# Four of 32 weight tiles converted in the first feed-forward block instead of in the last two attention pairs

## The chip, the cores and the metric

The kernel runs on one core of a Trainium2 chip. The metric is the device time of one execution in microseconds, as the median of several runs. TensorE (PE in the profile) multiplies matrices, VectorE (DVE), ScalarE (ACT) and GpSimd (POOL) do elementwise work, and SyncE (SP) issues nearly all DMA transfers. Each engine works off its own list of instructions in order.

## What is computed

Attention with a bucket mask over 4 batches, 8 heads, 768 positions and a head size of 64, followed by a feed-forward part with a rational function in place of an activation:

```python
mask = q_bucket[:, :, :, None] == k_bucket[:, :, None, :]
scores = np.where(mask, scale * np.matmul(q, k.transpose(0, 1, 3, 2)), -1000000000.0)
attn = np.exp(scores - np.max(scores, axis=-1, keepdims=True))
attn = attn / (np.sum(attn, axis=-1, keepdims=True) + 1e-09)
x = np.matmul(attn, v)            # put together to 3072 tokens x 512

h = x @ w_in                      # 512 x 2048
P = a[0] + a[1] * h + a[2] * h * h + a[3] * h * h * h
Q = 1.0 + np.abs(b[0]) * np.abs(h) + np.abs(b[1]) * h * h
out = (P / (Q + 1e-6)) @ w_out    # 2048 x 512
```

The two weight matrices arrive as 64-bit floating-point numbers. q, k, v and the rest are 32-bit.

## The kernel before

**Attention.** The 32 heads of all batches are worked off as 16 pairs. For each pair TensorE computes the row maxima (tile psm), which VectorE reduces (m); the maxima are transposed (pst) and moved as one more row into the operand q, so that they are subtracted within the product. Then come the scores (pss), their exponentials on ScalarE (E), partial sums of the exponentials on GpSimd (acc; in the last pair partly on VectorE), the sums (psu) and the product with the values (psv). The order of all of this is written out: a table `plan` gives each piece a position, 12 positions to a pair, and the pieces are emitted in the order of these positions. Since every instruction is pinned in program order, that order is the order of each engine's list and of SP's list of transfers.

**Weights.** The two matrices are cut into 32 tiles of 128 x 512. Tile n with an even number is a piece of w_in: (n/2) divided by 4 gives the column block and the row block. Tile n with an odd number is the row block (n-1)/2 of w_out. Every tile has to be turned from 64-bit into 32-bit numbers and then split into a high part, in the reduced format that TensorE multiplies at full speed, and a low part, the rest. `weights(i)` (line 432) does it in steps: a load of 512 KB into wr; a ScalarE copy of the upper words to ws; a ScalarE copy of the lower words together with a VectorE instruction that keeps the sign; a VectorE instruction that shifts and joins; a VectorE addition (in the profile a custom instruction on 128 x 1024 half words); a ScalarE copy that gives the high part; a VectorE subtraction that gives the low part. The parts of w_in stay on the chip, in wi_hi and wi_lo. Those of w_out are stored to the tensor wo_d in HBM (a seventh or eighth step) and fetched later. Lines 522 to 527 spread these steps over the plan, two tiles to a pair of heads; tiles 28 and 29 stand in pair 14, 30 and 31 in pair 15, partly in the pair behind. Tile 31 has four closer positions for its last steps (`weights_last`, line 47).

**Tokens.** `Tokens.load` (line 637) fetches the attention's outputs for one block of 512 tokens in three chunks c, multiplies them by the reciprocals of the sums (y = x * r on VectorE) and splits the result into high and low parts (xh on ScalarE, xl on VectorE). y lies in the places lo0 and lo1 in turn. A block's tokens are made in the block before; in step f = 3, 7, 11 a chunk is loaded, two steps later y is computed and one step after that xh and xl.

**Feed-forward part.** Six blocks of 512 tokens, 16 column tiles f each: 96 steps. `Ffn.step(i)` (line 748) emits, for step i, the first product of tile i (psh, 12 matmuls), the polynomials of tile i (`terms`: three ScalarE and three VectorE instructions), the quotient of tile i-1 (`quotient`: two and three), the split of tile i-2 (`parts`: gh on ScalarE, gl on GpSimd) and the second product of tile i-4 (`gemm2`, pso, 12 matmuls: for each of four row blocks gh with the high part of the weights, gh with the low part, gl with the high part). psh has four places, and gh and gl have three each.

Steps 0 to 2 of the first block are emitted within the plan, at the end of attention. `Ffn.rest` (line 761) emits what is left. It sets up 16 places wo0 to wo15 for the tiles of w_out, in memory that attention has used, issues the loads of wo0 to wo5, and then in each step i from 3 on one load more (wo6 in step 3, wo15 in step 12). In steps 3, 6 and 7 it also advances the last store of sums and the last reciprocals.

Of the kernel before, what the change touches and what calls it, by code (L numbers as in the profile page):

```python
# [18 lines left out]
P = 128  # L19
# [80 lines left out]
    (queue or nc.sync).dma_start(out.bitcast(F32), in_.bitcast(F32))  # L100


@with_exitstack
def bucket_attention_then_rational_ffn(ctx, tc, qT, kT, v, proj, w_in, w_out, coef, consts, out):
    nc = Ordered(tc)
    nc.scalar.preload_act_table_set("natural_log_exp_and_others")

    cpool = ctx.enter_context(tc.tile_pool(name="cpool", bufs=1))
    dpool = ctx.enter_context(tc.tile_pool(name="dpool", bufs=1, space=DRAM))
    wpool = ctx.enter_context(tc.tile_pool(name="wpool", bufs=1))  # L110


    raw = ctx.enter_context(tc.tile_pool(name="raw", bufs=2))
    ps_b = ctx.enter_context(tc.tile_pool(name="ps_b", bufs=1, space=PSUM))
    QF, KF = {}, {}
# [24 lines left out]
    r_d = [dpool.tile([2 * NHP, S], F32, name=f"r_d{i}") for i in range(B)]  # L140

    wo_d = [dpool.tile([P, 2, DM], F32R, name=f"wo_d{i}") for i in range(NFC)]

    wi_hi = wpool.tile([P, NCC, DFF], F32R, name="wi_hi")
    wi_lo = wpool.tile([P, NCC, DFF], F32R, name="wi_lo")

    tokens = Tokens(tc, nc, raw, x_d, r_d)
    gemm = Gemm1(nc, ps_b, tokens, wi_hi, wi_lo)
    tail = ctx.enter_context(tc.tile_pool(name="tail", bufs=1))

    def coefficients():
        nc.sync.dma_start(ab, coef)
        yield
        nc.scalar.activation(absb1, b1, AF.Abs)
        yield

    early = ExitStack()
    right = ctx.enter_context(ExitStack())
    ffn = Ffn(tc, nc, tokens, gemm, wo_d, (a0, a1, a2, a3, b0, absb1, qbias), tail, out)
# [13 lines left out]
def attention(ctx, tc, nc, raw, ps_b, tail, tokens, early, operands_to_terms, ffn, load, QF, KF, v, w_in, w_out, wo_d, ident, cst, ones, prj,  # L173
# [256 lines left out]
        yield  # L430

    def weights(i):

        if i % 2 == 0:
            f, cc = divmod(i // 2, 4)
            sl = slice(f * 512, f * 512 + 512)
            src, hi, lo = w_in[cc * P : cc * P + P, sl], wi_hi[:, cc, sl], wi_lo[:, cc, sl]
        else:  # L440
            src, hi, lo = w_out[i // 2 * P : i // 2 * P + P, :], None, None
        r = sm.tile([P, 2 * 512], F32, tag="wr", name=f"wr{i}", bufs=2)
        t = sm.tile([P, 512], F32, tag="ws", name=f"ws{i}", bufs=2)
        if src.dtype == F32:
            nc.sync.dma_start(t, src)
            yield
        else:
            nc.sync.dma_start(r.bitcast(I32), src.bitcast(I32))
            yield
            hw, lw = r[:, 1:1024:2], r[:, 0:1024:2]  # L450
            nc.scalar.activation(t, hw, AF.Copy, scale=2.0 ** -112)
            yield
            nc.scalar.activation(lw.bitcast(I32), lw.bitcast(U32), AF.Copy, scale=2.0 ** -29)
            nc.vector.tensor_scalar(out=hw.bitcast(I32), in0=hw.bitcast(I32), scalar1=-(1 << 31), scalar2=None,
                                    op0=ALU.bitwise_and)
            yield
            nc.vector.scalar_tensor_tensor(out=t.bitcast(I32), in0=t.bitcast(I32), scalar=3, in1=hw.bitcast(I32),
                                           op0=ALU.logical_shift_left, op1=ALU.bitwise_or)
            yield
            nc.vector.tensor_tensor(out=t.bitcast(I32), in0=t.bitcast(I32), in1=lw.bitcast(I32), op=ALU.add)  # L460
            yield
        if hi is None:
            hi, lo = r[:, 0:512].bitcast(F32R), r[:, 512:1024].bitcast(F32R)
        nc.scalar.copy(hi, t)
        yield
        nc.vector.tensor_tensor(out=lo, in0=t, in1=hi.bitcast(F32), op=ALU.subtract)
        yield
        if i % 2 == 1:
            move(nc, wo_d[i // 2], r.rearrange("p (t c) -> p t c", t=2))
            yield  # L470

# [11 lines left out]
    for p in range(NPAIR):  # L483
# [133 lines left out]
class Tokens:  # L617
# [19 lines left out]
    def load(self, t, c):  # L637
        nc = self.nc
        hi, lo = self.place(t, c, "h"), self.place(t, c, "l")
        w = hi.shape[1]  # L640
        x, r = lo.bitcast(F32), hi.bitcast(F32)
        o = 0
        while o < w:
            cc, k = divmod(c * S + o, NTK)
            bb, a = divmod(t * NTK + k, S)
            n = min(S - a, NTK - k, w - o)
            nc.sync.dma_start(x[:, o : o + n], self.x_d[bb * NHP + cc][:, a : a + n])
            for j in range(2):
# [12 lines left out]

class Ffn:
# [1 line left out]

    LAG = 4

    def __init__(self, tc, nc, tokens, gemm, wo_d, coef, rows, out):
        self.tc, self.nc, self.tokens, self.gemm, self.wo_d, self.coef, self.out = tc, nc, tokens, gemm, wo_d, coef, out
        self.rows = rows
        self.state, self.sums = {}, {}  # L670
        self.done = 0
# [89 lines left out]
    def rest(self, ctx, last):  # L761
# [70 lines left out]
```

## Time and profile before

| | us |
|---|---|
| runs of the kernel | 930.82, 931.18, 933.48; median 931.18 |
| the profiled execution | 931.52 |
| its span, first to last instruction | 929.7 |
| TensorE busy | 920.8 |
| VectorE busy | 840.8 |
| ScalarE busy | 647.7 |
| GpSimd busy | 436.5 |

The granted TensorE clock is 1.00. Attention fills the span up to about 401 us and the feed-forward part the rest. "Busy" for TensorE includes overlaps of matmuls that follow each other, so its share doesn't say that TensorE works at its peak. The profile gives line 93, that of the helper which pins the order, for nearly all instructions; groups are told apart by their tiles (psh is the first product, pso the second, and so on). Views by time give the start, the duration, the engine and the group, and in brackets how long the engine had been idle and what ended it.

### The profile page before, as it was taken

How to read it: one execution, taken by the hardware profiler on the slowest of the kernel's cores; microseconds unless marked ns; L12 is line 12 of the kernel's file. 1: busy time of each engine (PE TensorE's matmuls, PEld its weight loads, DVE VectorE, ACT ScalarE, POOL GpSimd, SP SyncE). 2: the span in 40 equal slices, each digit the busy share in tenths (PEclk: the TensorE clock that was granted, in tenths of full speed). 3: DMA queues.
4: the chain of work that ended last, by engine and by line, in shares of the span. 5: the costliest groups of instructions: out<-in, count | busy, mean ns of one | idle time of the engine just before them, and what ended most of it. 6: DMA issues, size and time to landing. Idle time of an engine off the chain costs nothing.

```text
span 929.7 us, 13698 instructions
## 1 busy us (share of the span) xinstructions
PE 920.8 (99%) x4678; PEld 699.3 (75%) x4678; DVE 840.8 (90%) x1029; ACT 647.7 (70%) x1229; POOL 436.5 (47%) x362
## 2 busy tenths in 40 slices
PE   8999999999999999999999999999999999999997
PEld 4666766666767676668888888888888888888886
DVE  6799889788988897887998999999999989998996
ACT  7567767676767676886777667776676677677664
POOL 5587878777878877622222232222223222222222
PEclk9999999999999999999999999999999999999999
DMA  6867877887877777545402100400040003001001
GB/s 197 213 182 225 229 221 230 214 232 220 232 218 220 220 193 228 166 158 189 165 1 86 51 1 1 136 1 0 1 137 1 1 38 98 1 1 46 1 1 46
DMA packets 51242, 111.57 MB, mean 120 GB/s; under 512 B 9346, under 2 KB 20214, under 8 KB 51172
## 3 DMA queue, kind: packets, MB, share of 16 engines
q1 hardware_dynamic: 50740, 110.47, 40.2%
q8 instruction: 37, 0.61, 0.3%
q14 instruction: 33, 0.27, 0.1%
q10 hardware_dynamic: 432, 0.23, 0.1%
HBM read 56.82 MB, written 21.17 MB: 84 GB/s over the span
## 4 chain that ended last, share of the span: by engine, by line
PE 92%; DVE 3%; DMA 3%; SPq 1%; issue 1%; ACT 1%; DVEq 0%; ACTq 0%
PE psh L93 28%; PE pso L93 28%; PE pss L93 13%; PE psv L93 12%; PE psm L93 7%; PE psu L93 2%; DVE m L93 2%; PE psb L93 1%; SPq L93 1%; DMA wr<-w_in 1%; DMA q<-q 1%; DVE ws L93 1%; DVE wr L93 0%; DMA qkf<-kT 0%; DMA xh<-r_d 0%
## 5 line engine op out<-in xcount | busy, mean ns | idle before, releaser
L93 POOL TENSOR_TENSOR gl<-c,gh 128x512 fp32r<-128x512 f32 x96 | 134.6, 1402 | 388.3 <-ACT gh L93 378.9
L93 ACT ACTIVATE E<-pss 128x384 f32<-128x384 f32 x384 | 167.7, 493 | 104.3 <-PE pss L93 93.8
L93 PE MATMUL pso<-wo,gh 128*128 128x512 f32 x768 | 235.5, 389 | 0.0
L93 DVE TENSOR_REDUCE m<-psm 128x1 f32<-128x768 f32 x192 | 179.4, 948 | 30.7 <-PE psm L93 27.6
L93 POOL TENSOR_TENSOR acc<-E,E 128x384 f32<-128x384 f32 x124 | 154.1, 1261 | 84.5 <-ACT E L93 84.4
L93 PE MATMUL pss<-q,k 128*128 128x384 f32 (+2 forms) x768 | 171.2, 346 | 0.4 <-ACT E L93 0.3
L93 PEld LDWEIGHTS pso<-wo,gh 128*128 128x128 f32 x768 | 144.1, 188 | 29.9
L93 PEld LDWEIGHTS pss<-q,k 128*128 128x128 f32 (+2 forms) x768 | 134.5, 189 | 29.2 <-issue 17.0
L93 PE MATMUL psh<-xh,wi_hi 128*128 128x512 f32 x384 | 149.6, 390 | 0.0
L93 PE MATMUL psh<-xl,wi_hi 128*128 128x512 f32 x384 | 149.4, 389 | 0.0
L93 PE MATMUL psh<-xh,wi_lo 128*128 128x512 f32 x384 | 149.4, 389 | 0.0
L93 PE MATMUL pso<-wo,gl 128*128 128x512 f32 x384 | 148.4, 389 | 0.0
L93 ACT ACTIVATE h<-psh 128x512 f32<-128x512 f32 x96 | 57.4, 598 | 127.5 <-PE psh L93 127.4
L93 POOL TENSOR_TENSOR acc<-acc,E 128x384 f32<-128x384 f32 x123 | 137.5, 1137 | 8.2 <-ACT E L93 8.0
L93 DVE SCALAR_TENSOR_TENSOR c<-c,ab,r 128x512 f32<-128x512 f32 x96 | 135.6, 1413 | 0.0
L93 PE MATMUL psv<-E,v 128*64 128x385 f32 x768 | 133.0, 492 | 0.0
L93 PE MATMUL psm<-k,q 76*128 76x384 f32 (+1 forms) x384 | 102.1, 349 | 1.9 <-DVE m L93 1.0
L93 PEld LDWEIGHTS psv<-E,v 128*64 128x64 f32 x768 | 52.4, 136 | 66.3 <-issue 63.2
L93 DVE SCALAR_TENSOR_TENSOR w<-h,absb,w 128x512 f32<-128x512 f32 x96 | 74.0, 771 | 16.1 <-ACT w L93 15.9
L93 PEld LDWEIGHTS psh<-xh,wi_hi 128*128 128x128 f32 x384 | 72.0, 187 | 16.2 <-issue 1.2
L93 PEld LDWEIGHTS psh<-xl,wi_hi 128*128 128x128 f32 x384 | 72.1, 188 | 15.0
L93 PEld LDWEIGHTS pso<-wo,gl 128*128 128x128 f32 x384 | 72.1, 188 | 15.0
(79 smaller groups left out, 1219.4 us busy)
## 6 DMA issues: line engine op xcount, KB each, us to landing
q<-q SPq DMA_DIRECT2D x45, 192.0 KB
k<-k SPq DMA_DIRECT2D x45, 192.0 KB
wr<-w_in SPq DMA_DIRECT2D x16, 512.0 KB
wr<-w_out SPq DMA_DIRECT2D x16, 512.0 KB
wo_d<-wr SPq DMA_DIRECT2D x16, 512.0 KB
wo<-wo_d SPq DMA_DIRECT2D x16, 512.0 KB
qkf<-qT SPq DMA_DIRECT2D x16, 384.0 KB
qkf<-kT SPq DMA_DIRECT2D x16, 384.0 KB
```

The source lines that it names most:

```text
L93: return self.tc.keep_in_program_order(issue(*args, **kwargs))
```

## The change

Tiles 28 to 31 (the last two row blocks of w_in in its last column block, and the last two row blocks of w_out) are no longer in attention's plan. The body of `weights` becomes a function `convert`, used in both places. In `Ffn.rest` a table gives the steps in which the pieces of the four tiles are emitted, behind the step's own work: for tile 28 the load ahead of step 3 (behind the loads of wo0 to wo5), the first copy in step 3, and so on to the subtraction in step 7; tile 30 in steps 4 to 10, tile 29 in 7 to 13, tile 31 in 8 to 15. The tables hold one number for each of the seven pieces: load, copy, lower words and sign, join, addition, high part, low part.

The 64-bit words lie in places of w_out tiles that come later: 28 and 29 in wo15, 30 and 31 in wo13. The 32-bit numbers lie in lo1 (28 and 31), wo14 (30) and wo12 (29); lo1 is free since y now lies in lo0 always. The low part is computed on GpSimd instead of VectorE. Tiles 29 and 31 are written straight into wo14 and wo15 and aren't stored to wo_d, which has 14 tiles now. wo6 to wo11 are loaded in steps 3 to 8 as before, wo12 and wo13 in step 14 (before: steps 9 and 10).

```diff
-    weights_last=[0.5, 0.8, 1.0, 1.2],
...
+def convert(nc, src, hi, lo, buffers, kept=None, last=None):
+    r, t = buffers()
...
+    nc.scalar.copy(hi, t)
+    yield
+    (last or nc.vector).tensor_tensor(out=lo, in0=t, in1=hi.bitcast(F32), op=ALU.subtract)
+    yield
+    if kept is not None:
+        move(nc, kept, r.rearrange("p (t c) -> p t c", t=2))
+        yield
...
-    for i in range(2 * NFC):
+    for i in range(2 * NFC - 4):
         o = 12 * (i // 2)
         w = list(FIRST["weights"][i]) if i < 2 else list(MID["weights"][i % 2])
-        if i == 2 * NFC - 1:
-            w = w[:-4] + [w[-5] + x for x in MID["weights_last"]]
         spread(0, [o + x for x in w], weights(i))
...
-        y = self.raw.tile([P, w], F32, tag=f"lo{c % 2}", name=f"y{t}_{c}", bufs=1)
+        y = self.raw.tile([P, w], F32, tag="lo0", name=f"y{t}_{c}", bufs=1)
...
-        self.wo = [wp.tile([P, 2, DM], F32R, name=f"wo{i}") for i in range(NFC)]
-        AHEAD = 6
+        self.wo = {}
+
+        def second(f):
+            self.wo[f] = wp.tile([P, 2, DM], F32R, tag=f"wo{f}", name=f"wo{f}")
+            return self.wo[f]
+
+        def late(n, r, t):
+            def buffers():
+                return (wp.tile([P, 2 * 512], F32, tag=f"wo{r}", name=f"wr{n}"),
+                        tokens.raw.tile([P, 512], F32, tag="lo1", name=f"ws{n}", bufs=1) if t is None else
+                        wp.tile([P, 512], F32, tag=f"wo{t}", name=f"ws{n}"))
+
+            if n % 2 == 0:
+                yield from convert(nc, *parts_of_w_in(n // 2, self.w_in, self.gemm.hi, self.gemm.lo), buffers, last=nc.gpsimd)
+            else:
+                yield from convert(nc, self.w_out[n // 2 * P : n // 2 * P + P, :], lambda: second(n // 2), None, buffers, last=nc.gpsimd)
+
+        AHEAD, LATE = 6, {}
+        for n, r, t, steps in ((28, 15, None, (2, 3, 4, 4, 5, 6, 7)), (30, 13, 14, (4, 6, 7, 7, 8, 9, 10)),
+                               (29, 15, 12, (7, 9, 10, 10, 11, 12, 13)), (31, 13, None, (8, 11, 12, 12, 13, 14, 15))):
+            g = late(n, r, t)
+            for i in steps:
+                LATE.setdefault(i, []).append(g)
         for f in range(AHEAD):
-            move(nc, self.wo[f], self.wo_d[f])
+            move(nc, second(f), self.wo_d[f])
         start = self.done
+        for g in LATE[start - 1]:
+            next(g)
         for i in range(start, NBLK * NFC + self.LAG):
             f = i - start + AHEAD
-            if f < NFC:
-                move(nc, self.wo[f], self.wo_d[f])
+            if f < NFC - 4:
+                move(nc, second(f), self.wo_d[f])
             t, f = divmod(i, NFC)
             self.step(i)
+            for g in LATE.get(i, ()):
+                next(g, None)
+            if i == 14:
+                for f2 in (NFC - 4, NFC - 3):
+                    move(nc, second(f2), self.wo_d[f2])
```

More of the change, by code (lines that the diff above doesn't have):

```diff
@@ L100, in move, with parts_of_w_in @@
     (queue or nc.sync).dma_start(out.bitcast(F32), in_.bitcast(F32))
+def parts_of_w_in(n, w_in, wi_hi, wi_lo):
+    f, cc = divmod(n, NCC)
+    sl = slice(f * 512, f * 512 + 512)
+    return w_in[cc * P : cc * P + P, sl], wi_hi[:, cc, sl], wi_lo[:, cc, sl]
+def convert(nc, src, hi, lo, buffers, kept=None, last=None):
+    r, t = buffers()
+    if src.dtype == F32:
+        nc.sync.dma_start(t, src)
+        yield
+    else:
+        nc.sync.dma_start(r.bitcast(I32), src.bitcast(I32))
+        yield
+        hw, lw = r[:, 1:1024:2], r[:, 0:1024:2]
+        nc.scalar.activation(t, hw, AF.Copy, scale=2.0 ** -112)
+        yield
+        nc.scalar.activation(lw.bitcast(I32), lw.bitcast(U32), AF.Copy, scale=2.0 ** -29)
+        nc.vector.tensor_scalar(out=hw.bitcast(I32), in0=hw.bitcast(I32), scalar1=-(1 << 31), scalar2=None,
+                                op0=ALU.bitwise_and)
+        yield
+        nc.vector.scalar_tensor_tensor(out=t.bitcast(I32), in0=t.bitcast(I32), scalar=3, in1=hw.bitcast(I32),
+                                       op0=ALU.logical_shift_left, op1=ALU.bitwise_or)
+        yield
+        nc.vector.tensor_tensor(out=t.bitcast(I32), in0=t.bitcast(I32), in1=lw.bitcast(I32), op=ALU.add)
+        yield
+    if hi is None:
+        hi, lo = r[:, 0:512].bitcast(F32R), r[:, 512:1024].bitcast(F32R)
+    elif callable(hi):
+        w = hi()
+        hi, lo = w[:, 0, :], w[:, 1, :]
+    nc.scalar.copy(hi, t)
+    yield
+    (last or nc.vector).tensor_tensor(out=lo, in0=t, in1=hi.bitcast(F32), op=ALU.subtract)
+    yield
+    if kept is not None:
+        move(nc, kept, r.rearrange("p (t c) -> p t c", t=2))
+        yield
 @with_exitstack
@@ L140, in bucket_attention_then_rational_ffn @@
     r_d = [dpool.tile([2 * NHP, S], F32, name=f"r_d{i}") for i in range(B)]
-    wo_d = [dpool.tile([P, 2, DM], F32R, name=f"wo_d{i}") for i in range(NFC)]
+    wo_d = [dpool.tile([P, 2, DM], F32R, name=f"wo_d{i}") for i in range(NFC - 2)]
     wi_hi = wpool.tile([P, NCC, DFF], F32R, name="wi_hi")
@@ L158, in bucket_attention_then_rational_ffn @@
     right = ctx.enter_context(ExitStack())
-    ffn = Ffn(tc, nc, tokens, gemm, wo_d, (a0, a1, a2, a3, b0, absb1, qbias), tail, out)
+    ffn = Ffn(tc, nc, tokens, gemm, (w_in, w_out, wo_d), (a0, a1, a2, a3, b0, absb1, qbias), tail, out)
     def operands_to_terms():
@@ L432, in weights @@
     def weights(i):
+        def buffers():
+            return (sm.tile([P, 2 * 512], F32, tag="wr", name=f"wr{i}", bufs=2), sm.tile([P, 512], F32, tag="ws", name=f"ws{i}", bufs=2))
         if i % 2 == 0:
[L437 to L470, printed above, removed]
+            return convert(nc, *parts_of_w_in(i // 2, w_in, wi_hi, wi_lo), buffers)
+        return convert(nc, w_out[i // 2 * P : i // 2 * P + P, :], None, None, buffers, wo_d[i // 2])
     plan = {}
@@ L665, with __init__ @@
     LAG = 4
-    def __init__(self, tc, nc, tokens, gemm, wo_d, coef, rows, out):
-        self.tc, self.nc, self.tokens, self.gemm, self.wo_d, self.coef, self.out = tc, nc, tokens, gemm, wo_d, coef, out
+    def __init__(self, tc, nc, tokens, gemm, weights, coef, rows, out):
+        self.tc, self.nc, self.tokens, self.gemm, self.coef, self.out = tc, nc, tokens, gemm, coef, out
+        self.w_in, self.w_out, self.wo_d = weights
         self.rows = rows
@@ L765, in rest, with buffers @@
         self.ps_o = ctx.enter_context(tc.tile_pool(name="ps_o", bufs=4, space=PSUM))
-        self.wo = [wp.tile([P, 2, DM], F32R, name=f"wo{i}") for i in range(NFC)]
-        AHEAD = 6
+        self.wo = {}
[3 more added lines that the diff above has]
+        def late(n, r, t):
+            def buffers():
+                return (wp.tile([P, 2 * 512], F32, tag=f"wo{r}", name=f"wr{n}"),
[3 more added lines that the diff above has]
+                yield from convert(nc, *parts_of_w_in(n // 2, self.w_in, self.gemm.hi, self.gemm.lo), buffers, last=nc.gpsimd)
+            else:
+                yield from convert(nc, self.w_out[n // 2 * P : n // 2 * P + P, :], lambda: second(n // 2), None, buffers, last=nc.gpsimd)
[5 more added lines that the diff above has]
+                LATE.setdefault(i, []).append(g)
         for f in range(AHEAD):
-            move(nc, self.wo[f], self.wo_d[f])
+            move(nc, second(f), self.wo_d[f])
         start = self.done
+        for g in LATE[start - 1]:
+            next(g)
         for i in range(start, NBLK * NFC + self.LAG):
             f = i - start + AHEAD
-            if f < NFC:
-                move(nc, self.wo[f], self.wo_d[f])
+            if f < NFC - 4:
+                move(nc, second(f), self.wo_d[f])
             t, f = divmod(i, NFC)
             self.step(i)
+            for g in LATE.get(i, ()):
[3 more added lines that the diff above has]
+                    move(nc, second(f2), self.wo_d[f2])
             if i in (3, 6, 7):
```

## The prediction

> **What bounds the kernel now.** I read the page first, then the chain of work that ended last in order of time, around the place of the change and to the end.
>
> ```profile
> span 929.7 us, 13698 instructions
> ```
>
> ```profile
> 331.25 4.03 PE psv L93 x24
> ...
> 343.48 4.03 PE psv L93 x24
> ...
> 349.48 0.35 PE psm L93 x2
> ...
> 354.36 4.08 PE psv L93 x24
> ...
> 377.37 4.03 PE psv L93 x24
> ...
> 383.71 1.43 PE psu L93 x16
> ...
> 387.45 4.03 PE psv L93 x24
> ...
> 396.73 4.03 PE psv L93 x24
> ...
> 410.59 5.71 PE psh L93 x24
> 416.30 2.72 PE pso L93 x12
> ...
> 911.34 12.94 PE pso L93 x57
> ```
>
> TensorE sets the end. In the feed-forward part each step is 12 matmuls of the first product and 12 of the second, 2.72 us each, 5.44 us together. From 416.30 to 911.34 are 495.04 us, which is 91 such steps to the hundredth: not one stall. Nothing there can become faster by moving conversions, and every wait that TensorE gets there is added to the time.
>
> In attention the chain is TensorE too, with gaps. I measure gaps by comparing equal work. Between the starts of two groups of 24 value matmuls (psv), with sums inside: 331.25 to 343.48, 12.23 us; without sums: 343.48 to 354.36, 10.88 us.
>
> ```profile
> 366.80 4.74 PE L93 MATMUL psv<-E,v 128*64 128x385 f32 x24
> ...
> 375.01 0.28 PE L93 MATMUL pst<-cst,m 128*12 128x128 f32 x1 [0.49 <-DVE m L93]
> ```
>
> ```profile
> 368.60 0.68 ACT L93 ACTIVATE ws<-wr 128x512 f32<-128x512 f32 x1 [2.38 <-DMA wr<-w_in]
> ...
> 394.31 0.63 ACT L93 CAST wi_hi<-ws 128x512 fp32r<-128x512 f32 x1
> 394.82 2.41 ACT L93 ACTIVATE E<-pss 128x384 f32<-128x384 f32 x6
> ```
>
> ```profile
> 369.32 0.43 DVE L93 TENSOR_SCALAR wr<-wr 128x512 int32<-128x512 int32 x1 [2.78 <-ACT ws L93]
> ```
>
> Three gaps follow the start of the work that is moved. (a) 354.36 to 366.80 with sums: 12.44, 0.21 too long. (b) 366.80 to 377.37: 10.57. This stretch has five maxima pairs fewer than the one of 10.88; a pair (psm) takes 0.35, so 9.1 would do: 1.4 lost. The rows say why: ScalarE stands 2.38 us at the load of tile 28, VectorE 2.78 us behind ScalarE, and the last maxima, queued behind tile 28 on VectorE, hold TensorE's transpose (pst). (c) 387.45 to 396.73: 9.28; the stretch before it, 377.37 to 387.45, has the same work plus one group of sums (1.43): 8.65. So 0.63 lost, in a stretch where ScalarE's exponentials of consecutive scores follow each other without idle time and tile 30's copy to wi_hi stands among them. Together 0.21 + 1.4 + 0.63 = 2.25 us. After 396.73 TensorE runs through.
>
> **The change part by part.** *Removed from the last two pairs:* for tiles 28 to 31 four loads, two stores to wo_d, twelve ScalarE and sixteen VectorE instructions.
>
> ```profile
> L93 ACT ACTIVATE ws<-wr x32: 664/675/759, 31.9 to 397.1; 128x512 f32<-128x512 f32 x32
> L93 ACT ACTIVATE wr<-wr x32: 669/686/769, 32.4 to 397.6; 128x512 int32<-128x512 uint32 x32
> L93 DVE TENSOR_SCALAR wr<-wr x32: 409/422/1558, 32.8 to 398.7; 128x512 int32<-128x512 int32 x32
> L93 DVE SCALAR_TENSOR_TENSOR ws<-ws,wr x32: 678/1370/1493, 46.1 to 400.3; 128x512 int32<-128x512 int32 x32
> L93 DVE CUSTOM_DVE_ANT_0 ws<-wr,ws x32: 669/681/1461, 49.6 to 401.0; 128x1024 uint16<-128x1024 uint16 x32
> ```
>
> Only what lies in the gaps counts. (a) and (b) go with tile 28: without its load ScalarE isn't held, and VectorE, without that wait and tile 28's instructions, reaches the maxima when TensorE delivers them. In (c) ScalarE is freed of one copy, at an issue pitch of 0.51 us (394.31 to 394.82), so about 0.5 of the 0.63 goes. Gain: 0.21 + 1.4 + 0.5 = 2.1 us; bounds 0 (something else is late at the same places) and 2.25 (all three). The order of TensorE's own instructions isn't changed, so no more is to be had: 2.25 us is 0.24% of the time.
>
> The halved use of lo0/lo1 (y always in lo0) costs nothing here: y, xh and xl of one chunk are done before the next y, all in VectorE's order.
>
> *Added: the first load.* Tile 28's load is issued behind wo0 to wo5, before wo6, and ScalarE's first instruction on it stands at the end of step 3, ahead of all of step 4.
>
> ```profile
> 411.03 3.38 SPq L93 DMA_DIRECT2D wo<-wo_d  x7
> ...
> 423.66 0.32 SPq L93 DMA_DIRECT2D rs<-s_d  x1
> ...
> 430.57 2.01 SPq L93 DMA_DIRECT2D wo<-wo_d  x4
> ```
>
> ```profile
> GB/s 0 0 0 0 22 153 175 240 317 393 382 437 426 361 382 382 404 382 426 426 382 459 404 426 426 382 481 393 404 426 219 74 33 22 8 0 0 44 3 59
> ```
>
> The second fence is the DMA rate from 410 to 425 us, 0.375 us a figure. Seven transfers of 512 KB run at about 400 GB/s, 1.3 us each, and the seventh ends at about 421.4. In the new kernel the seventh is tile 28, so (in the time of the old profile) it lands there, seen by ScalarE at about 421.9, with 421.4 and 423.7 as bounds (the latter: SP saw the stores of sums, behind the same seven, only at 423.66).
>
> ```profile
> 417.15 0.59 ACT L93 ACTIVATE h<-psh 128x512 f32<-128x512 f32 x1
> ...
> 418.66 0.78 ACT L93 ACTIVATE c<-psh,ab 128x512 f32<-128x512 f32 x1 [0.33 <-POOL gl L93]
> ...
> 420.62 0.60 ACT L93 CAST gh<-c 128x512 fp32r<-128x512 f32 x1
> ```
>
> ```profile
> 421.30 1.30 POOL L93 TENSOR_TENSOR gl<-c,gh 128x512 fp32r<-128x512 f32 x1 [2.68 <-ACT gh L93]
> ...
> 439.09 1.30 POOL L93 TENSOR_TENSOR gl<-c,gh 128x512 fp32r<-128x512 f32 x1 [6.83 <-ACT gh L93]
> ```
>
> Step 4 on ScalarE (three terms, two of the quotient, then gh of tile 2) began at 417.15. Now it begins after the landing and one copy, 421.9 + 0.57 = 422.5: 5.3 later, less about 0.4 for the wait on gl that is absorbed (0.33 and its wake-up), 4.9. So gl of tile 2, done at 422.60, is done at 427.5. The second product of tile 2 starts two steps after 416.30, at 427.18, and takes gl with its third matmul, 0.45 later at 427.63, its weights 0.2 before that. TensorE stalls about 0.1 to 0.3 us, and one more us for each us of later landing (up to 2.1 at 423.7).
>
> By a rule of the Trainium skill ("DMA: Bandwidth & Descriptors", "Where 436 GB/s comes from") transfers from HBM are held to some 358 GB/s per core; as an estimate, seven of 524,288 B would then need 10.3 us from the first byte, land about a microsecond later, and the sum would come out near 930.6. The trace disagrees: its figures stand at 361 to 481 GB/s.
>
> *Added: tile 30's load* is second behind wo7 after the token loads, at 430.57. All of that is 1.3 us later by tile 28's place in the queue (SP waits for the stores of sums behind it), and the token loads ahead of it were there when VectorE began y, at 433.31 (row below); so tile 30 lands around 433.3 + 1.3 + 2 x 1.3 = 437.2. ScalarE's copy of it stands ahead of xh.
>
> ```profile
> 434.31 0.84 ACT L93 CAST xh<-y 128x768 fp32r<-128x768 f32 x1 [3.46 <-DMA wo<-wo_d]
> ```
>
> So ScalarE goes on at about 437.2 + 0.57 = 437.8 instead of 434.31, 3.5 later. gl of tile 5, done at 440.39, would be done at 443.9; it is needed for the third matmul of 443.50, at 443.95 less 0.2. Stall 0.1 to 0.2, 2 at a landing of 439. Both stalls shift TensorE as a whole, so the first lends slack to the second: I take 0.5 us for both, bounds 0 and 3.
>
> *Added on VectorE:* twelve instructions in steps 4 to 13, at least 4 x (0.42 + 0.68 + 0.68) = 7.1 us, at most 4 x (1.56 + 1.49 + 1.46) = 18. The four subtractions go to GpSimd, at 1.30 each like gl (same shape).
>
> ```profile
> 433.31 0.96 DVE L93 TENSOR_TENSOR y<-xl,xh 128x768 f32<-128x768 f32 x1 [4.54 <-DMA xh<-r_d]
> ...
> 445.16 0.75 DVE L93 SCALAR_TENSOR_TENSOR w<-h,absb,w 128x512 f32<-128x512 f32 x1
> ...
> 449.20 0.74 DVE L93 SCALAR_TENSOR_TENSOR w<-h,absb,w 128x512 f32<-128x512 f32 x1
> ...
> 460.11 1.84 DVE L93 SCALAR_TENSOR_TENSOR w<-h,absb,w 128x512 f32<-128x512 f32 x1
> ...
> 493.70 0.75 DVE L93 SCALAR_TENSOR_TENSOR w<-h,absb,w 128x512 f32<-128x512 f32 x1 [0.27 <-ACT w L93]
> ```
>
> VectorE idles 4.54 us at the first y: tile 28's three instructions fit there, and y itself comes 1.3 later. Behind it VectorE is late until 493.70, but a late step takes it 4.04 us (445.16 to 449.20) against TensorE's 5.44: 1.4 to spare in each step. Steps 7 to 13 spare 9.8 us; they get nine instructions, 5.3 us by the lower prices, 13.5 by the upper ones, beside the token work that was there already.
>
> ```profile
> 460.11 1.30 POOL L93 TENSOR_TENSOR gl<-c,gh 128x512 fp32r<-128x512 f32 x1 [4.71 <-ACT gh L93]
> ```
>
> This gl, of tile 9, ended at 461.41 and was wanted at 416.30 + 9 x 5.44 + 0.45 = 465.71: 4.3 us of slack, more than the 3.7 by which the upper prices go over. I take no stall here.
>
> A subtraction on GpSimd still costs VectorE: w took 1.84 where gl started with it, 0.75 alone, so 0 to 1.09 for each of the four. The Trainium skill ("SBUF — State Buffer", "SBUF: two separate sides") says that the two share a pair of ports as an exclusive lock, so the move relieves VectorE less than it seems; with 4.4 us instead of nothing the spare time would be used up and the sum, as an estimate, up to 1 us higher. The trace agrees with the lock.
>
> Tiles 12 and 13 come from wo_d after step 14 and are wanted at steps 16 and 17, over 8 us later; a transfer takes 1.3. Nothing.
>
> *Sum.* The profiled execution took 931.52 us, its span and 1.82 around it; it lies 0.34 above the median of 931.18. 931.52 - 2.1 + 0.5 = 929.92; against the median, 929.6.
>
> **The rivals.** *A: the late load eats the gain.* Tile 28 lands at 423.7 instead of 421.9, or tile 30 at 439: cost 2 to 3 us, 931 to 932. For it: SP's 423.66. Against: the rate falls off at 421.4.
>
> *B: slower, by ScalarE's queue.* One load that isn't there blocks all of ScalarE behind it, hence gh, gl and TensorE. Break-even with the gain of 2.1 is a landing at about 423.7; at 426.7 the kernel is 0.3% slower. It would be so if the transfers ran at the rate that the page shows for most of attention:
>
> ```profile
> GB/s 197 213 182 225 229 221 230 214 232 220 232 218 220 220 193 228 166 158 189 165 1 86 51 1 1 136 1 0 1 137 1 1 38 98 1 1 46 1 1 46
> ```
>
> At 225 GB/s one takes 2.33 us, seven 16.3 from the first byte at about 411.9; seen at 428.7, 6.8 later than I take it, a stall of 7.0: 931.18 - 2.1 + 7.0 = 936.1. Against it: 400 GB/s in this very place.
>
> *C: no gain.* Another late operation (the token products on VectorE, SP's long list) fills gap (b): gain 0.5 at most, cost 0.5: 931.2.
>
> *D: all of the gain and no cost:* 931.18 - 2.25 = 928.9.
>
> **How the numbers follow.** Forecast (gain about 2, cost up to 1.2: 929.0 to 930.5) 0.48; A 0.17; B 0.15; C 0.10; D, with what lies below it, 0.10. About 0.3% (2.8 us) is what a measurement of this kernel can tell from no change. Only a part of D, with a gain beyond the gaps that I found, is faster by more: 0.10. B is slower by more, 0.15. The rest, 0.75, is within. The range takes in D, the forecast, A and C and leaves out most of B: 928.4 to 933.2. Predicted: 929.6.
>
> **What would show it.** Right: the chain has TensorE alone between 366 and 377 and the distance of psv starts there falls to about 9.1; psh starts 2 us earlier than 400.76; ScalarE's first copy ws<-wr in the feed-forward part waits 4 to 5 us for a DMA; VectorE is late until step 18 without holding TensorE. Wrong: gaps of TensorE in steps 6 to 12 of more than 1 us together, waits of psh on wi_lo in steps 12 to 15, or a gap at 374 that stays.

## The result, and the profile after

| | before | after |
|---|---|---|
| median of the runs made side by side, us | 932.31 (6 runs, 930.82 to 934.79) | 943.60 (6 runs, 942.25 to 947.60) |
| the profiled execution, us | 931.52 | 942.25 |
| its span, us | 929.7 | 940.5 |

The ratio is 1.0124, with an interval of 1.0100 to 1.0149: the changed kernel is slower by 1.2%. The prediction of 929.6 us, and its whole range, was too low. In the profile of the changed kernel the helper's line is 92 instead of 93.

The chain of work that ended last, of the changed kernel, in order of time (start, duration, work):

```profile
353.70 4.03 PE psv L92 x24
366.91 4.03 PE psv L92 x24
376.28 4.03 PE psv L92 x24
...
386.36 4.03 PE psv L92 x24
...
395.13 4.03 PE psv L92 x24
399.16 8.38 PE psh L92 x36
...
435.01 1.71 DVE w L92
...
442.99 1.69 DVE w L92
...
488.11 0.69 DVE c L92
489.46 1.22 PE psh L92 x2
490.68 4.08 PE pso L92 x12
494.76 2.72 PE psh L92 x12
```

Two things are to be seen. The first psh starts at 399.16, 1.60 us earlier than 400.76 before: the gain in attention is there. But from 433 to 489 the chain now runs almost wholly through VectorE (and from 409 to 433 through transfers). TensorE is back on it only at 489.46, with a psh.

How much is lost behind the first psh can be measured without knowing any wait, as the distance from the first psh to the kernel's last VectorE instruction. The rows of the timeline for the one and of the chain for the other, before:

```profile
400.69 0.49 PE L93 MATMUL psh<-xh,wi_hi 128*128 128x512 f32 x1
```
```profile
925.69 0.42 DVE oh L93
```

and after:

```profile
399.09 0.50 PE L92 MATMUL psh<-xh,wi_hi 128*128 128x512 f32 x1
```
```profile
936.15 0.42 DVE oh L92
```

That is 525.00 us before and 537.06 after: **12.06 us lost in the feed-forward part.** With the 1.60 gained, and 0.3 more behind the last instruction shown, it makes the 10.8 by which the span grew. I call this distance, less 525.00, the loss of a kernel; every experiment below is read by it. It comes from one profile of each kernel, the ratios from all of its runs. The first psh itself starts anywhere between 398.4 and 400.8 us in the nine profiles of the changed kernel and its variants, so their spans alone would mislead.

Where TensorE stood, from the view of its waits between 414 and 505 us (sum, times, longest), after:

```profile
PE psh L92 <- DVE xl L92: 4.5, 1, 4.5
PE pso L92 <- POOL gl L92: 2.2, 3, 0.8
PE psh L92 <- POOL wi_lo L92: 1.1, 1, 1.1
PE pso L92 <- ACT gh L92: 0.2, 1, 0.2
```

A group of twelve matmuls takes 2.72 us. Eight groups took longer, by the distance of their starts in the timeline: those at 422.67 and 425.75 by 0.36 and 1.15 (1.51 together), those at 445.94, 448.77, 455.41 and 459.05 by 0.11, 1.20, 0.92 and 1.36 (3.59), those at 482.20 and 490.48 by 5.56 and 1.40 (6.96). The sum is 12.06, all of the loss. The last pair is more than half of it, and it begins with a wait for xl, the low part of the next block's tokens. The timeline of TensorE there, after:

```profile
489.46 0.80 PE L92 MATMUL psh<-xl,wi_hi 128*128 128x512 f32 x1 [4.52 <-DVE xl L92]
```

The xl that it waited for, on VectorE, before:

```profile
477.96 0.69 DVE L93 TENSOR_TENSOR xl<-y,xh 128x512 fp32r<-128x512 f32 x1
```

and after:

```profile
488.72 0.68 DVE L92 TENSOR_TENSOR xl<-y,xh 128x512 fp32r<-128x512 f32 x1
```

This xl belongs to the last row block of block 1's tokens, and the 11th matmul of step 16 is the first to need it. Before, step 5's psh started at 419.02, behind the first pso of 416.30 and 2.72, and step 16's 11 steps of 5.44 later, at 478.86; ten matmuls further is 481.13, and its weights are wanted 0.2 earlier: 80.2 us behind the first psh of 400.76. xl was done after 77.9 us, with 2.3 to spare. In the changed kernel it was done after 90.2, 12.3 later.

Why VectorE was so late is seen in the rows of VectorE and GpSimd around one inserted pair. VectorE, before:

```profile
444.55 0.69 DVE L93 SCALAR_TENSOR_TENSOR c<-w,c 128x512 f32<-128x512 f32 x1
445.16 0.75 DVE L93 SCALAR_TENSOR_TENSOR w<-h,absb,w 128x512 f32<-128x512 f32 x1
445.82 0.68 DVE L93 TENSOR_TENSOR c<-psh,c 128x512 f32<-128x512 f32 x1
```

VectorE, after:

```profile
447.37 0.69 DVE L92 SCALAR_TENSOR_TENSOR c<-w,c 128x512 f32<-128x512 f32 x1
447.98 0.42 DVE L92 TENSOR_SCALAR wr<-wr 128x512 int32<-128x512 int32 x1
448.43 0.69 DVE L92 SCALAR_TENSOR_TENSOR ws<-ws,wr 128x512 int32<-128x512 int32 x1
449.04 1.76 DVE L92 SCALAR_TENSOR_TENSOR w<-h,absb,w 128x512 f32<-128x512 f32 x1
```

GpSimd, before, and then after:

```profile
446.03 1.30 POOL L93 TENSOR_TENSOR gl<-c,gh 128x512 fp32r<-128x512 f32 x1 [5.64 <-ACT gh L93]
```
```profile
448.85 1.41 POOL L92 TENSOR_TENSOR gl<-c,gh 128x512 fp32r<-128x512 f32 x1 [4.71 <-PE psh L92]
```

Once c of a tile is done, ScalarE makes gh in about 0.6 us, and then GpSimd starts gl. Before, VectorE passes from c straight to w of the next tile, w is over when gl starts (446.03), and gl lies beside instructions that take one operand from psh. After, 1.1 us of tile 30's instructions stand between c and w; gl starts at 448.85, w at 449.04 and takes 1.76 instead of 0.75. So this inserted pair costs its 1.1 us and another 1.0. The pairs of tiles 29 and 31 do the same (behind them an xl takes 2.05 us and a w 1.78); that of tile 28 doesn't (w 0.74).

Over all of VectorE's rows from the first psh to that xl: the twelve instructions take 6.7 us (4 x (0.46 + 0.61 + 0.60), from start to start); what instructions take above their time alone is 4.0 us before and 9.9 after, so 5.9 more (nearly all of it in four instructions before and ten after that are held by more than 0.2 us, 3.5 and 9.6 us); the waits are 0.2 less. Together 12.4, which is what xl was later, but for the rounding.

### The profile page after: what moved, and what is told of

It is laid out like the page before. It is cut to its first block, busy times and chain, and to the rows that moved or that the text cites. A ratio compares the mean times of both kernels' runs of the same rounds, so it can differ in the third digit from the quotient of the medians.

```text
span 940.5 us, 13697 instructions
## 1 busy us (share of the span) xinstructions
PE 923.4 (98%) x4678; PEld 700.1 (74%) x4678; DVE 841.9 (90%) x1025; ACT 648.3 (69%) x1229; POOL 447.0 (48%) x366
## 4 chain that ended last, share of the span: by engine, by line
PE 86%; DVE 8%; DMA 3%; SPq 1%; issue 1%; ACT 0%; DVEq 0%
PE pso L92 24%; PE psh L92 24%; PE pss L92 14%; PE psv L92 13%; PE psm L92 7%; DVE c L92 2%; PE psu L92 2%; DVE m L92 2%; DVE w L92 2%; PE psb L92 1%; DMA wo<-wo_d 1%; DVE ws L92 1%; DMA s_d<-sr 1%; SPq L92 1%; DMA wr<-w_in 1%
## 5 line engine op out<-in xcount | busy, mean ns | idle before, releaser
L92 POOL TENSOR_TENSOR gl<-c,gh 128x512 fp32r<-128x512 f32 x96 | 137.9, 1436 | 391.4 <-ACT gh L92 361.5
L92 DVE SCALAR_TENSOR_TENSOR w<-h,absb,w 128x512 f32<-128x512 f32 x96 | 77.0, 802 | 23.8 <-ACT w L92 23.6
```

The costliest lines, as they stand in the source:

```text
L92: return self.tc.keep_in_program_order(issue(*args, **kwargs))
```

## The experiments

**Theory:** VectorE's time decides. What is inserted makes the chain of quotients and tokens late, and TensorE waits wherever that chain has a due time. **Rivals:** ScalarE's hold at the first load costs most of it; the subtractions on GpSimd do; only the place of one due time is wrong.

| kernel | loss, us | ratio to before | interval |
|---|---|---|---|
| the changed kernel | 12.06 | 1.0124 | 1.0100 to 1.0149 |
| 1 attention's half alone | 0.02 | 0.9965 | 0.9944 to 0.9986 |
| 2 first load ahead of wo0 to wo5 | 8.74 | 1.0076 | 1.0053 to 1.0100 |
| 3 VectorE's pieces between terms and quotient | 8.85 | 1.0076 | 1.0052 to 1.0100 |
| 4 low parts on VectorE | 10.96 | 1.0099 | 1.0079 to 1.0120 |
| 5 six of the twelve VectorE instructions left out | 5.78 | 1.0035 | 1.0021 to 1.0049 |
| 6 block 1's third token chunk earlier | 9.15 | 1.0058 | 1.0039 to 1.0078 |
| 7 edits 2, 3, 4 and 6 together | 1.19 | 0.9993 | 0.9982 to 1.0003 |
| 8 as 7, and block 1's first token chunk loaded earlier | 0.26 | 0.9987 | 0.9978 to 0.9996 |

**1. Attention's half alone.** Tiles 28 to 31 are not converted at all: the places of the two w_in parts and of wo14 and wo15 are filled by plain transfers of other tiles, so that part of the output isn't computed. All that left attention is gone, and nothing is added on VectorE. (The diffs from here on are against the changed kernel and show its main lines.)

```diff
-        for g in LATE[start - 1]:
-            next(g)
...
-            for g in LATE.get(i, ()):
-                next(g, None)
+            if i == 8:
+                for cc in (2, 3):
+                    move(nc, self.gemm.hi[:, cc, 1536:2048], self.wo_d[0][:, 0, :])
+                    move(nc, self.gemm.lo[:, cc, 1536:2048], self.wo_d[0][:, 1, :])
             if i == 14:
-                for f2 in (NFC - 4, NFC - 3):
-                    move(nc, second(f2), self.wo_d[f2])
+                for f2 in range(NFC - 4, NFC):
+                    move(nc, second(f2), self.wo_d[min(f2, NFC - 3)])
```

> The attention half alone: tiles 28 to 31 leave attention's plan and are not converted at all (their places are filled by plain transfers of other tiles, so this part of the computation is left out). The changed kernel's first pso stood 1.64 us earlier than before (414.66 against 416.30). If the removal is a gain by itself and all of the loss sits in the feed-forward part: 1.6 to 2 us below the kernel before, ratio 0.998. If the removal is worth nothing on the end (rival): ratio 1.000. If attention's new arrangement itself costs something later: above 1.002.

Measured: 930.38 against 932.95 us; no wait of TensorE in the feed-forward part. The chain:

```profile
354.38 4.03 PE psv L92 x24
...
366.87 4.03 PE psv L92 x24
...
399.05 8.43 PE psh L92 x36
```

From 354.38 to 399.05 are 44.67 us, 1.73 less than before's 46.40 (354.36 to 400.76). Of the other eight profiles five show 1.7 as well, and three (the changed kernel, experiments 4 and 8) 0.9 to 1.0, although the work in attention is the same in all nine. So taking the work out of attention is worth one or the other in a profile, and all of the loss comes from the other half of the change.

**2. The first load ahead.** Tile 28's load goes ahead of wo0 to wo5.

```diff
-        for f in range(AHEAD):
-            move(nc, second(f), self.wo_d[f])
         start = self.done
         for g in LATE[start - 1]:
             next(g)
+        for f in range(AHEAD):
+            move(nc, second(f), self.wo_d[f])
```

> Only the place of tile 28's load: ahead of wo0 to wo5 instead of behind them. It should land about 7 us earlier, so that ScalarE isn't held for 5.9 us at the end of step 3. Theory 1 (VectorE's lateness at xl, step 14, decides; ScalarE's block is only one of its sources, the first y being bound to its own transfers at about 431.4 anyway): VectorE is about 2.7 us earlier at y and stays so, the kernel gains 2 to 3 us on the changed one, ratio to before about 1.009. Theory 2 (the block of ScalarE's queue is the root of the whole loss): nearly all of 12 us comes back, ratio 0.998 to 1.002. Theory 3 (the early stalls of TensorE and the late one are independent): the 1.5 us of the first stall, ratio 1.011.

Measured: the loss falls by 3.3 us, to 8.74, somewhat more than expected. TensorE's waits:

```profile
PE psh L92 <- DVE xl L92: 4.5, 1, 4.5
PE psh L92 <- POOL wi_lo L92: 1.1, 1, 1.1
```

The waits for gh and gl are gone, the one for xl is still 4.5 us: xl is done 3.4 us earlier, counted from the first psh (VectorE waits 1.3 less ahead of it, and its held instructions lose 2.1 less), but TensorE, not held up before it, comes for it earlier too. ScalarE's hold at the first load is a part of the loss, and not the larger one.

**3. Between terms and quotient.** The same instructions in another order: sign, join and addition of a tile, with the ScalarE copy of the lower words that goes with the sign, stand behind the three terms of a step instead of behind the quotient, so that w follows c again at once.

```diff
+            for k, i in enumerate(steps):
+                (VECTOR if k in (2, 3, 4) else LATE).setdefault(i, []).append(g)
...
-            self.step(i)
+            self.step(i, VECTOR.get(i, ()))
```

> Only the place, within a step, of the three VectorE pieces of each tile (with the ScalarE copy that goes with the first): between the polynomials and the quotient instead of behind the quotient. Work, steps and transfers are the same. In the changed kernel an extra VectorE instruction behind the quotient pushes the next w (two inputs in SBUF) into the 1.3 us in which GpSimd computes gl, and w takes 1.7 to 1.8 us instead of 0.75, seven times before the late xl; between the two, gl should fall on instructions that read psh and aren't held. Theory 1 with this collision as a main term: 4 to 5 us less than the changed kernel, ratio about 1.007, and few w above 1 us. If the amount of work alone counts (rival): no difference from the changed kernel, ratio 1.012.

Measured: the loss falls by 3.2 us, to 8.85, somewhat less than the 4 to 5 expected. VectorE and GpSimd around the same pair of tile 30, in this kernel:

```profile
444.40 0.42 DVE L92 TENSOR_SCALAR wr<-wr 128x512 int32<-128x512 int32 x1
444.86 0.69 DVE L92 SCALAR_TENSOR_TENSOR ws<-ws,wr 128x512 int32<-128x512 int32 x1
...
447.46 0.74 DVE L92 SCALAR_TENSOR_TENSOR w<-h,absb,w 128x512 f32<-128x512 f32 x1
```
```profile
448.34 1.28 POOL L92 TENSOR_TENSOR gl<-c,gh 128x512 fp32r<-128x512 f32 x1 [4.08 <-ACT gh L92]
```

w is done at 448.20, before gl starts, and takes 0.74. No instruction is missing. The late xl is done 3.0 us earlier, 2.4 of it because held instructions lose less (eight are still held, instead of ten) and 0.6 because VectorE waits less. So this part of the loss is due to the place alone.

**4. Low parts on VectorE.** The four subtractions go back from GpSimd to VectorE.

```diff
-                yield from convert(nc, *parts_of_w_in(n // 2, self.w_in, self.gemm.hi, self.gemm.lo), buffers, last=nc.gpsimd)
+                yield from convert(nc, *parts_of_w_in(n // 2, self.w_in, self.gemm.hi, self.gemm.lo), buffers)
...
-                yield from convert(nc, self.w_out[n // 2 * P : n // 2 * P + P, :], lambda: second(n // 2), None, buffers, last=nc.gpsimd)
+                yield from convert(nc, self.w_out[n // 2 * P : n // 2 * P + P, :], lambda: second(n // 2), None, buffers)
```

> Only the engine of the four low parts: VectorE instead of GpSimd. If moving them to GpSimd relieved VectorE (rival): three more instructions of 0.6 us ahead of the late xl, 2 us or more slower than the changed kernel, ratio 1.014. If GpSimd holds VectorE while it computes them (theory 1: 1.04 us lost at tile 28's and at tile 30's, against 0.6 for each on VectorE): no difference or up to 1 us faster, ratio 1.011 to 1.012.

Measured: the loss is 10.96, 1.1 us less, although VectorE has four instructions more. The intervals of the two ratios overlap, so a gain is likely rather than certain; the 2 us or more that the rival would cost are ruled out. TensorE waits 3.4 us for xl instead of 4.5, but 2.7 instead of 1.1 for wi_lo, which VectorE now makes. Moving a subtraction of this shape to GpSimd didn't relieve VectorE here: in the changed kernel a subtraction on GpSimd took 1.3 to 2.0 us, and two of the three ahead of the late xl held up a VectorE instruction by about 1.0; on VectorE a subtraction takes 0.7 to 0.9 (experiment 8's profile).

**5. Six instructions fewer.** Sign, join and addition of tiles 29 and 31 are left out, so these two tiles of w_out aren't converted. All transfers, ScalarE's and GpSimd's instructions stay.

```diff
...
-        nc.vector.tensor_tensor(out=t.bitcast(I32), in0=t.bitcast(I32), in1=lw.bitcast(I32), op=ALU.add)
+        if joined:
+          nc.vector.tensor_tensor(out=t.bitcast(I32), in0=t.bitcast(I32), in1=lw.bitcast(I32), op=ALU.add)
...
```

The sign and the join are put behind the same condition, and the two tiles of w_out pass `joined=False`.

> The changed kernel with the six VectorE instructions of tiles 29 and 31 left out (sign, join, addition; so these two tiles of w_out hold wrong numbers); their loads, ScalarE copies and GpSimd subtractions stay. From the runs so far, the loss of the feed-forward part against the attention half alone (span 928.2) is the lateness of the last xl of step 14 beyond 80.2 us after the first psh, plus some 2 us of low clock. Theory 1 (that xl decides): it comes 5 to 6.5 us earlier (six instructions of 0.35 to 0.69 us, and two or three collisions of 1.04), so its lateness falls from 10 to about 4, the clock doesn't drop, and what is left is the early stalls of TensorE, 5.1 us: ratio 1.001 to 1.003. If the transfers, ScalarE's copies or GpSimd's subtractions were what holds TensorE (rival): no difference, 1.011 to 1.012.

Measured: the loss is 5.78, down by 6.3 us; the ratio lies just above the expected 1.001 to 1.003. TensorE's waits:

```profile
PE pso L92 <- POOL gl L92: 1.9, 3, 0.8
PE psh L92 <- POOL wi_lo L92: 1.1, 1, 1.1
PE psh L92 <- DVE xl L92: 1.0, 1, 1.0
```

Six instructions of 3.3 us in all take the wait for xl from 4.5 to 1.0 and leave the earlier waits as they were. So VectorE's time decides about xl, which is done 4.5 us earlier, counted from the first psh. That the loss fell by 6.3 has one more cause, which the last section shows.

**6. The tokens earlier.** Block 1's third token chunk is loaded in step 9 instead of 11, its y computed in step 11 instead of 13 and its xh and xl in step 12 instead of 14: the rival of one misplaced due time.

```diff
-                c, n = divmod(f - 3, 4)
...
+                for c, x, k in ({3: [(0, 0, 1)], 5: [(0, 1, 1)], 6: [(0, 1, 2)], 7: [(1, 0, 1)], 9: [(1, 1, 1), (2, 0, 1)], 10: [(1, 1, 2)],
+                                 11: [(2, 1, 1)], 12: [(2, 1, 2)]} if t == 0 else
...
+                    if x == 0:
+                        coming[c] = tokens.load(t + 1, c)
+                    for _ in range(k):
+                        next(coming[c])
```

> The changed kernel with the third chunk of block 1's tokens two steps earlier: load in step 9, y in 11, xh and xl in 12, instead of 11, 13 and 14; nothing else. The work on VectorE and its order otherwise are the same. Theory 1 (the deadline of that xl, needed by the 11th matmul of step 16, decides, and nothing behind it): the wait of 4.5 us and the low clock behind it go, the early stalls (5.1 us) stay: ratio 1.002 to 1.004. If VectorE's lateness is what counts wherever it is paid (rival): TensorE waits for gl in steps 16 to 18 instead, and the time stays at 1.010 to 1.012.

Measured: the loss is 9.15, between the two expectations; both fall in part. The waits of TensorE's weight loads:

```profile
PEld pso L92 <- POOL gl L92: 5.2, 5, 1.5
PEld pso L92 <- ACT gh L92: 2.0, 2, 1.4
PEld psh L92 <- POOL wi_lo L92: 1.5, 1, 1.5
```

The wait for xl is gone, and gl and gh are waited for longer (gl 3.5 and gh 1.0 in the same view of the changed kernel). About 1.6 us of the loss is low clock again, behind two of these waits (last section). VectorE lacks time; where its lateness is paid can be chosen, and only some of it is saved by choosing well.

**7. All four together.** 

```diff
+                (VECTOR if k in (2, 3, 4, 6) else LATE).setdefault(i, []).append(g)
```

with the edits of 2, 4 and 6 (the subtraction, piece 6, now lies between terms and quotient too).

> All of it together: tile 28's load ahead of wo0, the VectorE pieces between polynomials and quotient, the low parts on VectorE (also there), the third chunk of block 1's tokens two steps earlier. The output is complete. Theory 1: neither the early stalls nor the late one are left, and the kernel keeps attention's gain: ratio to before 0.996 to 0.999, faster than both kernels. If the added work can't be hidden in the first block at all (rival): above 1.002, with TensorE waiting for gl somewhere in steps 6 to 19.

Measured: 932.10 against 932.99 us, loss 1.19, 10.9 less than the changed kernel. The ratio lies just above the expected 0.996 to 0.999, and the kernel isn't told apart from before. Instructions of VectorE that are held lose 3.6 us up to 474, where this kernel's xl is done; before the change it was 3.5 and in the changed kernel 7.5 up to the same time. The single gains, 3.3, 3.2, 1.1 and 2.9, add up to 10.5. That this is so near to 10.9 is partly chance: each of the four kernels still pays for a low clock (1.6 to 2 us, last section), and this one doesn't. What is left:

```profile
PEld pso L92 <- POOL gl L92: 1.5, 4, 0.5
```

VectorE still waited 2.35 us for block 1's first token chunk, at 431.63.

**8. The first chunk too.** That chunk is loaded between wo1 and wo2, ahead of the stores of the sums, instead of in step 3.

```diff
         for f in range(AHEAD):
+            if f == 2:
+                coming[0] = tokens.load(1, 0)
+                next(coming[0])
             move(nc, second(f), self.wo_d[f])
```

> The kernel with all four moves (load of tile 28 first, pieces between terms and quotient, low parts on VectorE, block 1's third token chunk one step earlier), and block 1's first token chunk now loaded ahead of the stores of the sums, so that the y that waited 2.35 us for it does not wait. Theory (VectorE is the short resource, what it loses early is paid later in gl): the 2.35 us come back to VectorE before step 11, the four waits of 0.5 us on gl go in whole or in part (1.2 to 2.0 us together): ratio to before 0.9965 to 0.998, no wait of TensorE above 0.3 us between its first psh and the end. Rival (what is left are collisions of VectorE with GpSimd in the very steps where the low parts fall, not the backlog): the four waits stay, ratio 0.999.

Measured: 930.86 us (11 runs) against 931.81 (15 runs), ratio 0.9987 with an interval of 0.9978 to 0.9996. The loss is 0.26. TensorE's weight loads have one wait left, for ScalarE's r in the first pso:

```profile
PEld pso L92 <- ACT r L92: 0.4, 1, 0.4
```

In the trace the rival falls: the four waits for gl went with VectorE's idle time. The time alone doesn't decide: 0.9987 lies above what the theory gave, 0.9965 to 0.998, and next to the rival's 0.999, and the interval overlaps that of experiment 7. The profiled execution was the longest of its eleven; its first psh starts at 400.78, so it had nothing of attention's gain. (The third token chunk is two steps earlier here, as in 6 and 7, not one.) Of the versions that compute everything this one has the lowest ratio, about 1 us below before and, by the two ratios, 1.4% below the changed kernel.

## Why the prediction was wrong, point by point

**TensorE sets the end, and a stall in the feed-forward part is added in full:** right. The eight late groups add up to the loss to the hundredth.

**The gain in attention, 2.1 us with bounds 0 and 2.25:** near, and on the low side of it. Gap (b) fell from 10.57 to 9.37 (9.1 was taken), (c) from 9.28 to 8.77 (as taken). Gap (a) did not close. The prediction took its end, 366.80, from the timeline and its start from the chain, which shows the same groups 0.07 later; in the timeline alone (a) was 12.51 and (b) 10.50 before. Gap (a) is 12.5 in six of the nine later profiles, experiment 1 among them, so tile 28 doesn't make it. In the other three it is 13.2: in the changed kernel's TensorE waited 0.73 us there for a maximum, queued on VectorE behind a token product y of 1.57 us that took 1.01 before. From the psv at 354 to the first psh the changed kernel's profile gains 0.94, and experiment 1's 1.73.

**The first load:** the mechanism was right, with the size off within its bounds. A landing at 421.9 was taken, in the old profile's time. ScalarE's timeline of the changed kernel:

```profile
421.52 0.66 ACT L92 ACTIVATE ws<-wr 128x512 f32<-128x512 f32 x1 [5.89 <-issue]
```

The copy starts after 5.89 us of idle time, 22.4 behind the first psh; that is 423.1 in the old time, near the upper bound of 423.7. The stall was 1.51 us instead of 0.1 to 0.3, as in rival A. But the delay went on: VectorE stood 4.35 us behind ScalarE up to 423.28 and no longer waited at the first y, so the 4.54 us of idle time that were counted for tile 28 had been used up earlier. That is in experiment 2's 3.3 us, which are more than the stall. The second load, tile 30's, held nothing: ScalarE's copy of it starts at 434.80 without a wait.

**"I take no stall here", for VectorE's twelve instructions:** this is the step that failed. 8.74 us of the loss are left when the first load holds nothing (experiment 2). It failed in three places.

First, the spare time was already spent. The prediction counted 1.4 us to spare in each of steps 7 to 13, 9.8 in all. It is there, but VectorE used it before the change to catch up, until 493.70. The windows of the kernel before (length, then the busy time of PE, PEld, DVE, ACT and POOL, the clock, the DMA share and rate) have it in one row:

```profile
437.00:494.00 57.00, 57.00 (x253) 47.22 (x252) 55.77 (x79) 41.02 (x68) 14.64 (x11) 1.00 0.22 75
```

VectorE worked 55.77 of 57.00 us. There was hardly any spare time in this stretch, only slack against due times.

Second, the slack was checked against gl alone. gl of tile 9 had 4.3 us. The xl of step 14 had 2.3, and its first user wasn't looked up. Experiment 6 shows that this is not the whole: with xl in time, gl and gh were late.

Third, collisions were looked for in the wrong place. The price as such wasn't the mistake: the measured 12.6 us, 6.7 for the twelve instructions alone and 5.9 for holds, lie within the prediction's 7.1 to 18. But beside those prices it looked for holds only at the four subtractions on GpSimd, 0 to 1.09 us each, at most 4.4, and took none of it into the sum. The inserted VectorE instructions moved w onto gl as well. Experiment 3 gives 3.2 us back by order alone. The Trainium skill ("SBUF — State Buffer", "SBUF: two separate sides") says that whichever of the two engines starts first holds the ports for its whole instruction. The trace agrees: w took 1.76 us where gl had started 0.19 ahead of it. What the wait for xl cost beyond its own length, 1.9 us of low clock (last section), stood in no term either.

**Rival B, slower by ScalarE's queue:** its sign came true and its mechanism is only a part, as experiment 2 shows.

**What would show it wrong:** gaps of TensorE in steps 6 to 12 of more than 1 us and waits of psh for wi_lo were named, and both are there. The largest wait, psh for xl in step 16, was not on that list.

## What to carry to other kernels

Before adding work to an engine, ask in which stretch it is late, and in that stretch take its free time as next to zero: read its busy time there, and not the difference of two step times. Then list every consumer of what that engine makes, with its due time, and price the addition against the smallest slack, not against the one that comes to mind first. And look at what the inserted instruction pushes the next one onto: the same twelve instructions cost 3.2 us less in another place of the step.

## What the runs showed of the hardware

**A wait of TensorE can cost more than its length.** The windows of the changed kernel around the wait for xl (busy time of PE, PEld, DVE, ACT and POOL, then the granted clock):

```profile
484.00:488.00 4.00, 0.90 (x3) 0.19 (x1) 3.96 (x5) 3.37 (x6) 0.88 (x1) 0.83 0.38 131
488.00:492.00 4.00, 2.54 (x6) 2.06 (x7) 3.93 (x7) 1.90 (x4) 2.41 (x2) 0.50 0.00 0
492.00:496.00 4.00, 4.00 (x16) 3.19 (x16) 3.93 (x6) 2.43 (x4) 1.28 (x2) 0.82 0.01 4
```

Within the 4.52 us of waiting the granted clock fell to 0.50. The next pso group took 4.08 us instead of 2.72, and the two last psh matmuls 1.02 instead of 0.45: 1.9 us on top of the wait. In experiment 5, where the same wait was 1.0 us, it stayed at 1.00:

```profile
484.00:488.00 4.00, 3.27 (x14) 2.69 (x15) 3.96 (x6) 3.19 (x6) 2.90 (x2) 1.00 0.00 0
```

That is most of why leaving out 3.3 us of VectorE work saved 6.3.

The length of a single wait doesn't settle it, though. In experiment 6 no wait of TensorE was above about 1 us, but two of them came close together, and the clock fell there too. TensorE's rows, and the window behind them:

```profile
485.31 0.73 PE L92 MATMUL pso<-wo,gh 128*128 128x512 f32 x2 [0.99 <-ACT gh L92]
487.06 0.79 PE L92 MATMUL pso<-wo,gl 128*128 128x512 f32 x1 [1.02 <-POOL gl L92]
```
```profile
488.00:492.00 4.00, 4.00 (x14) 3.12 (x13) 3.93 (x7) 3.39 (x6) 1.97 (x2) 0.71 0.02 4
```

Windows of 0.25 us place the changes. In the changed kernel the clock was at half from 486.6 to 493.4: it fell 1.7 us behind the end of the last matmul (484.93) and stayed low for 6.8 us. It stayed low for 6.8 us in experiment 2 as well, and for 3.4 in experiments 3, 4 and 6. In the 3.4 us ahead of the fall TensorE had still been busy for 1.7 us in the changed kernel and for 1.6 in experiment 6. The Trainium skill ("TensorE: Matmul & The Clock Gate", "Part 1: The HAM clock gate") puts the fall to half rate behind some 3.4 us without work, and the rise behind about as long with work. The trace has 3.4 us, or twice that, as the time at half rate, but it doesn't agree that 3.4 us without work are needed. What exactly decides is not shown here.

**The eighth transfer counts.** The prediction had seven transfers land one behind the other. In the changed kernel tile 28's was the seventh, and wo6 was issued right behind it. The DMA rate from 408.4 to 423.4 us, 0.375 us a figure:

```profile
GB/s 0 0 0 0 98 153 295 339 360 404 415 426 317 317 339 339 350 371 350 415 393 448 404 404 437 404 426 404 393 437 415 426 415 284 175 49 22 44 0 0
```

It falls from 415 to 49 GB/s between 420.8 and 421.9, when all eight are nearly through, and ScalarE started on tile 28 only then, at 421.52. (The view names no releaser for this start.) That the seventh and the eighth shared the engines, and so ended together, fits the 1.2 us (one transfer takes 1.3) by which the landing was off; no run tested it by itself.
